# A rewritten instruction order, and one addition of the gate moved from VectorE to an accumulating transfer, in a linear-attention and gated-convolution kernel

## The chip, the cores and the metric

The kernel runs on one core of one Trainium2 chip. The metric is device time in microseconds. Below, PE is the matrix engine (matmuls; its weight loads are shown as PEld), DVE is VectorE, ACT is ScalarE, POOL is GpSimd, and SP is SyncE, which issues transfers.

## The reference

There are two parts, one behind the other. The first is linear attention for 8 batches and 8 heads, with 576 positions and 64 values per head, then an RMS norm per head:

```python
kv = np.einsum('bhsd,bhse->bhde', k, v)
out = np.einsum('bhsd,bhde->bhse', q, kv)
rms = np.sqrt(np.mean(out * out, axis=-1, keepdims=True) + 1e-06)
return (out / rms * g_norm)
```

The heads are put side by side, which gives x with 576 rows of 512 values per batch. The second part is a feed-forward network with a gate:

```python
h = np.maximum(x @ w_in, 0.0)                 # 512 -> 1024
for k in range(3):                            # hp is h with a zero row at either end
    conv_out += conv_w[k][None, None, :] * hp[:, k:k + S, :]
gate = 1.0 / (1.0 + np.exp(-conv_out))
return (h * gate @ w_out)                     # 1024 -> 512
```

## The kernel before

Features lie on partitions and positions run along the free axis from the norm on. The 1024 features of h are 8 blocks of 128 (`f`), and the batches go in pairs: most steps of the second part work on two batches at once.

The whole program is one list of steps, `ORDER`, a string of 852 tokens. A token such as `ab.4.2.2` names a function with its arguments (batch 4, two batches, block pair 2, that is blocks 4 and 5), and `@0` gives it a slot: a PSUM bank, a row buffer or a tap buffer. Each step issues its instructions when the list reaches it, and a chain of dependencies keeps every engine's instructions in that order. So the list sets what each engine does next, and an engine waits in order for whatever its next instruction needs. Transfers are issued from queues too: the loads of q, k, v and the weights on POOL (`Lq`, `Lk`, `Lv`, `Li`, `Lo`), the stores and the transposing transfers on SP (`st`, `sh`, `tq`, `kx`).

The steps that matter below:

- `kv` and `kz` build k^T v on PE; `kva` and `kvd` copy it to SBUF as `kvb`, on ACT or on DVE (the same function `kvc`, L414 and L416). `ot` and `ox` multiply with q.
- The norm of batches 0 to 3: `sq` squares on ACT (L509), `on` or `oq` sums the squares on PE with a matrix of ones (`on` with whole 128-row matmuls, L528; `oq` with four of 64 rows, L537), `nl` takes the reciprocal root on ACT (L545), `mo` multiplies on DVE (L556).
- The norm of batches 4 to 7 is done for two batches at a time: `ss` sums the squares on PE, `ln` takes the reciprocal root on ACT (L574), `sl` makes of it two bf16 parts on DVE, the tile `wparts` (L581 to L584), `sp` spreads these on PE over the rows (L593, with the matrix `spread`), and `mu` multiplies on DVE (L599).
- `hk`, `hs`, `hm` are x @ w_in on PE; `rp`, `rh`, `re` apply the relu on ACT (L665, L640, L619).
- The gate: `ta` multiplies one block of h by the outer two weights of the convolution on DVE (L681 and L682, into the two halves of a tap buffer `taps`), `aa` adds the two products of two blocks, shifted against each other (L687), `ab` adds h (L692, whose weight has been divided out), `sg` takes the sigmoid on ACT (L698), `mg` multiplies h by it (L722). There are two tap buffers.
- `om` is the product with w_out on PE (L732, 8 matmuls of 512 columns per tile of 128 rows, mostly given as two steps of four), `ea` or `ed` copies a tile to a row buffer, on ACT (L738) or DVE (L743), and `st` stores it. The last tile goes in two halves (`oh` L757, `eh` L767, `sh` L777). `fi` are filler matmuls on zeros (L286).

Of the kernel before, what the change touches and what calls it, by code (L numbers as in the profile page):

```python
# [54 lines left out]
AL = mybir.AluOpType  # L55
# [4 lines left out]
pre@0,1 af cad.q.0.0@0 cad.v.0.0@0 fi.10.512@0 qt.0.0.0@2 qd.0.0.0@0 gt.k.1.0 Li.0.4 fi.9.512@0 ct@0 Lq.1.0.2@1  # L60
Lk.1.0.2@0 Lv.1.0.2@1 Li.4.4 ps pg fi.4.512@1 cad.k.1.0@1 caa.v.1.0 caa.k.0.0 kv.0.0.1@4 kva.0.0.1@0 ot.0.0.0@6 pc
cad.v.3.0 cad.k.2.0 fi.2.512@0 cad.k.3.0 caa.q.1.0 qt.0.1.0@2 qd.0.1.0@1 sq.0.0.0@0 oq.0.0.0@4 fi.2.512@0 dg.1
caa.v.2.0 kv.0.1.1@0 fi.2.512@2 nl.0.0.0@0 kva.0.1.1 ot.0.1.0@4 sq.0.1.0@1 cad.q.0.1 qt.0.0.1@2 qa.0.0.1 fi.2.512@0
oq.0.1.0@0 nl.0.1.0@1 mo.0.0.0@0 cad.q.1.1 qt.0.1.1@6 qd.0.1.1 mo.0.1.0 ot.0.0.1@2 sq.0.0.1@2 ot.0.1.1@6 fi.1.512@0
sq.0.1.1@3 oq.0.0.1@0 nl.0.0.1@2 fi.1.512@4 fi.1.512@4 hk.0.1.0.0@4 hk.0.1.0.1 rp.1.0@0 on.0.1.1@0 nl.0.1.1@3
hk.0.2.0.0@5 hk.0.2.0.1 rp.2.0 dg.3 mo.0.0.1 dg.2 hk.0.3.0.0@4 hk.0.3.0.1 hk.0.0.0.0@2 hk.0.0.0.1 rp.0.0 hk.0.0.1.0@3
rp.3.0 hk.0.1.1.0@5 hk.0.3.1.0@0 mo.0.1.1 hk.0.3.1.1 rp.3.1 hk.0.1.1.1 rp.1.1 hk.0.0.1.1 rp.0.1 dg.0 hk.0.2.1.0@1
hk.0.2.1.1 qt.1.0.0@6 kv.1.0.1@4 rp.2.1 cv.0.2@2 sc.0.2@0 cv.0.3@0 qd.1.0.0@2 kvd.1.0.1@1 ot.1.0.1@6 sc.0.3 pl
sq.1.0.1@4 cv.0.1@4 cv.0.0@2 Lq.1.2.2 Lk.1.2.2 Lv.1.2.2 sc.0.1@1 fi.2.512@0 qt.1.1.0@0 qd.1.1.0@3 mg.0.1.1 Lo.0.8
sc.0.0 mg.0.1.0 oq.1.0.1@4 nl.1.0.1@4 mo.1.0.1@1 fi.1.512@2 hk.0.5.1.0@2 hk.0.5.0.0@3 hk.0.5.0.1 rp.5.0 hk.0.5.1.1  # L70
rp.5.1 ta.0.1.5@0 hk.0.4.1.0@0 hk.0.4.1.1 rp.4.1 hk.0.7.0.0@1 hk.0.7.0.1 kv.1.1.1@4 kvd.1.1.1 rp.7.0 ot.1.0.0@2
sq.1.0.0@5 hk.0.7.1.0@6 hk.0.7.1.1 rp.7.1 ta.0.1.7@1 ot.1.1.1@0 sq.1.1.1@6 oq.1.0.0@4 nl.1.0.0@5 mo.1.0.0 hk.0.4.0.0@6
hk.0.4.0.1 rp.4.0 hk.0.6.1.0@7 hk.0.6.1.1 rp.6.1 oq.1.1.1@4 nl.1.1.1@6 mo.1.1.1 hk.0.6.0.0@6 Lq.2.0.4@2 hk.0.6.0.1
rp.6.0 ta.0.1.4 hk.1.6.1.0@7 ta.0.1.6 hk.1.0.1.0@2 ot.1.1.0@4 sq.1.1.0@7 aa.0.1.2 hk.1.1.1.0@3 hk.1.2.1.0@6 hk.1.6.1.1
rh.1.6.1 hk.1.1.1.1 rh.1.1.1 on.1.1.0@0 nl.1.1.0@7 mo.1.1.0 hk.1.2.1.1 hk.1.5.1.0@7 hk.1.5.1.1 rh.1.5.1 rh.1.2.1
hk.1.3.1.0@3 hk.1.3.1.1 rh.1.3.1 hk.1.0.1.1 rh.1.0.1 ab.0.1.2 sg.0.1.5 sg.0.1.4 qt.2.1.0@0 qt.2.0.0@6 hk.1.5.0.0@3
hk.1.5.0.1 rh.1.5.0 qd.2.0.0@4 hk.1.0.0.0@2 hk.1.4.1.0@4 hk.1.4.1.1 hk.1.0.0.1 hk.1.1.0.0@5 hk.1.6.0.0@6 hk.1.1.0.1
hk.1.2.0.0@7 hk.1.2.0.1 rh.1.2.0 rh.1.1.0 rh.1.0.0 hk.1.6.0.1 rh.1.6.0 aa.0.1.3 qd.2.1.0@0 ab.0.1.3 sg.0.1.7 sg.0.1.6
hk.1.7.0.0@0 mg.0.1.2 hk.1.7.1.0@1 hk.1.7.1.1 rh.1.7.1 hk.1.7.0.1 rh.1.7.0 ta.1.1.1@0 ta.1.1.0 Lk.2.0.4@1 Lv.2.0.4@0
Lq.3.0.4@0 Lk.3.0.4@0 Lv.3.0.4@1 Lq.4.0.4@1 aa.1.1.0 hk.1.4.0.0@3 om.0.1.0.4@2 rh.1.4.1 hk.1.4.0.1 rh.1.4.0  # L80
om.0.2.0.4@5 kv.2.0.2@6 mg.0.1.3 om.0.1.4.4 ab.1.1.0 sg.1.1.0 sg.1.1.1 kvd.2.0.2@2 ot.2.0.1@0 sq.2.0.1@0 ed.0.1@0
# [57 lines left out]
def kernel(  # L139
# [685 lines left out]
```

## Time and profile before

| | before |
|---|---|
| median of three runs | 177.59 us (177.56 to 177.61) |
| span of the profiled execution | 175.6 us |
| what lies around the span, median less span | 1.99 us |
| PE busy | 167.9 us (96%) |
| DVE busy | 149.5 us (85%) |
| ACT busy | 148.9 us (85%) |
| POOL busy | 22.2 us (13%) |
| clock granted to PE | full speed in all slices |

The profile shows one execution. Its own time outside the span was not given apart, so the span stands beside the median. A profile row of a group reads: line, engine, operation, output <- input with its shape, count, then the busy total in us and the mean of one in ns, then the idle time of that engine just ahead and what ended it. A row of the timeline starts with its time from the start of the span and its length. A row of a stretch of time gives its start and end, its length, and the busy time of PE, PEld, DVE, ACT and POOL with their instructions, then the granted clock, the mean share of the DMA engines and GB/s.

### The profile page before, as it was taken

The numbers are of one execution on the slowest core, as the hardware profiler recorded it, in microseconds if no ns is written. First come the engines' busy times: TensorE is split into PE (matmuls) and PEld (weight loads), VectorE is DVE, ScalarE is ACT, GpSimd is POOL, SyncE is SP. The second block draws the span as 40 slices with busy tenths as digits, with TensorE's granted clock in tenths as the row PEclk, the third lists the DMA queues.
The fourth block names the chain that finished last, engine by engine and source line by source line (L and its number), as shares of the span: only waits on it lengthen the run. The fifth ranks groups of instructions, "written<-read, shape, count | busy, mean of one in ns | idle before, by whom it ended". The sixth has DMA issues, their size and how long they took to land.

```text
span 175.6 us, 5070 instructions
## 1 busy us (share of the span) xinstructions
PE 167.9 (96%) x2097; PEld 100.0 (57%) x2114; DVE 149.5 (85%) x290; ACT 148.9 (85%) x268; POOL 22.2 (13%) x35
## 2 busy tenths in 40 slices
PE   7979999999999999999999999999999999999992
PEld 2334766676447677644467764444877744444451
DVE  2796638899688899999999998989999999999950
ACT  2368899999978999999999998999999967676721
POOL 3094512200603013030000000000000000000000
PEclk9999999999999999999999999999999999999999
DMA  5999999999999999999999050330310003064486
GB/s 159 392 323 207 207 207 207 208 208 209 207 241 230 227 207 207 170 182 197 258 181 161 14 134 0 119 123 0 119 63 0 0 0 116 13 239 175 179 304 237
DMA packets 25911, 29.11 MB, mean 166 GB/s; under 512 B 6036, under 2 KB 20384, under 8 KB 25888
## 3 DMA queue, kind: packets, MB, share of 16 engines
q0 software_dynamic: 13296, 14.50, 49.2%
q1 hardware_dynamic: 12048, 13.11, 26.2%
q10 hardware_dynamic: 544, 1.18, 1.7%
q8 instruction: 16, 0.26, 0.6%
q14 instruction: 7, 0.06, 0.1%
HBM read 32.52 MB, written 9.44 MB: 239 GB/s over the span
## 4 chain that ended last, share of the span: by engine, by line
PE 76%; DVE 12%; ACT 5%; DMA 3%; issue 3%; ACTq 0%; DVEq 0%
PE banks L732 32%; PE banks L628 14%; PE banks L613 9%; PE banks L658 4%; DMA stg<-in_v_dram 3%; PE banks L460 3%; DVE h L722 2%; PE banks L708 2%; ACT taps L698 2%; PE banks L402 2%; PE banks L593 2%; PE banks L433 1%; PE banks L528 1%; DVE taps L681 1%; PE banks L286 1%
## 5 line engine op out<-in xcount | busy, mean ns | idle before, releaser
L732 PE MATMUL banks<-w_out_sb,h 128*128 128x512 bf16 x267 | 62.8, 379 | 1.2 <-issue 0.6
L698 ACT ACTIVATE taps<-taps,cw 128x576 bf16<-128x576 bf16 (+1 forms) x44 | 40.6, 958 | 5.7 <-DVE taps L692 5.5
L732 PEld LDWEIGHTS <-h 128*128 128x128 bf16 x280 | 26.2, 98 | 30.0 <-issue 1.1
L628 PE MATMUL banks<-x,w_in_sb 128*128 128x288 bf16 (+2 forms) x256 | 34.2, 286 | 0.0
L640 ACT ACTIVATE h<-banks 128x288 bf16<-128x288 f32 (+2 forms) x80 | 29.5, 460 | 0.3 <-PE banks L658 0.2
L628 PEld LDWEIGHTS <-w_in_sb 128*128 128x128 bf16 x256 | 24.4, 98 | 7.8 <-issue 0.8
L722 DVE TENSOR_TENSOR h<-h,taps 128x1152 bf16<-128x1152 bf16 (+1 forms) x24 | 22.8, 952 | 1.2 <-ACT taps L698 1.2
L687 DVE TENSOR_TENSOR taps<-taps 128x1152 bf16<-128x1152 bf16 (+1 forms) x22 | 21.5, 978 | 0.5
L509 ACT ACTIVATE sq<-banks 128x576 bf16<-128x576 f32 (+2 forms) x32 | 20.8, 691 | 1.1 <-PE banks L460 1.1
L692 DVE TENSOR_TENSOR taps<-taps,h 128x1152 bf16<-128x1152 bf16 (+1 forms) x22 | 21.4, 972 | 0.3
L681 DVE TENSOR_SCALAR taps<-h,cw 128x576 bf16<-128x576 bf16 (+1 forms) x44 | 18.7, 424 | 0.6 <-ACT h L665 0.5
L682 DVE TENSOR_SCALAR taps<-h,cw 128x576 bf16<-128x576 bf16 (+1 forms) x44 | 18.4, 418 | 0.0
L738 ACT ACTIVATE row<-banks 128x512 f32<-128x512 f32 x23 | 13.5, 597 | 5.7 <-PE banks L732 4.2
L658 PE MATMUL banks<-x,w_in_sb 128*128 128x288 bf16 (+2 forms) x128 | 17.7, 286 | 0.1
L613 PE MATMUL banks<-x,w_in_sb 128*128 128x288 bf16 x128 | 16.9, 286 | 0.0
L556 DVE SCALAR_TENSOR_TENSOR x<-banks,cw,rs 128x576 bf16<-128x576 f32 (+2 forms) x16 | 13.0, 816 | 3.9 <-ACT rs L545 3.6
L658 PEld LDWEIGHTS <-w_in_sb 128*128 128x128 bf16 x128 | 12.0, 98 | 4.4 <-issue 0.5
L227 ACT ACT_TABLE_LOAD x10 | 12.8, 1283 | 2.0 <-issue 1.8
L613 PEld LDWEIGHTS <-w_in_sb 128*128 128x128 bf16 x128 | 12.3, 98 | 3.7 <-issue 0.2
L443 DVE COPY qT<-banks 128x1152 bf16<-128x1152 bf16 (+2 forms) x13 | 8.8, 681 | 5.7 <-PE banks L433 5.7
L545 ACT ACTIVATE rs<-banks,eps_sb 128x576 f32<-128x576 f32 (+2 forms) x16 | 11.8, 740 | 1.1 <-PE banks L528 1.1
L599 DVE SCALAR_TENSOR_TENSOR x<-o,cw,banks 128x576 bf16<-128x576 f32 (+2 forms) x16 | 12.1, 810 | 0.7 <-PE banks L593 0.5
(89 smaller groups left out, 162.9 us busy)
## 6 DMA issues: line engine op xcount, KB each, us to landing
out_dram<-row SPq DMA_DIRECT2D x35, 256.0 KB, 2.3
q_sb<-in_q_dram POOLq DMA_DIRECT2D x6, 576.0 KB, 17.9
k_sb<-in_k_dram POOLq DMA_DIRECT2D x6, 576.0 KB, 14.5
v_sb<-in_v_dram POOLq DMA_DIRECT2D x6, 576.0 KB, 17.9
stg<-in_v_dram ACTq DMA_DIRECT2D x2, 576.0 KB, 6.2
stg<-in_k_dram SPq DMA_DIRECT2D x4, 288.0 KB, 6.9
w_in_sb<-in_moe_w_in_dram POOLq DMA_DIRECT2D x2, 512.0 KB, 9.9
w_out_sb<-in_moe_w_out_dram POOLq DMA_DIRECT2D x1, 1024.0 KB, 15.5
```

The costliest lines, as they stand in the source:

```text
L509: nc.scalar.activation(T["sq", b, u, s], T["o", b, u, s], AX.Square)
L613: nc.tensor.matmul(ps[:, s, :HS], w_in_sb[:, t, f * P:(f + 1) * P], T["x", b][:, t, c0:c1], start=(t == 0), stop=(t == NT - 1))
L628: nc.tensor.matmul(ps, w_in_sb[:, t, f * P:(f + 1) * P], T["x", b][:, t, c0:c1], start=(t == 0), stop=(t == NT - 1))
L640: nc.scalar.activation(h, fr, AX.Relu)
L658: nc.tensor.matmul(T[at], w_in_sb[:, t, f * P:(f + 1) * P], T["x", b][:, t, c0:c1], start=(t == 0), stop=(t == NT - 1))
L681: nc.vector.tensor_scalar_mul(tap[:, 0, f % 2, :n, 8:8 + S], h[:, f], cw[:, f:f + 1])
L682: nc.vector.tensor_scalar_mul(tap[:, 1, f % 2, :n, :S], h[:, f], cw[:, 2 * NF + f:2 * NF + f + 1])
L687: nc.vector.tensor_add(tap[:, 1, :, :n, :S], tap[:, 0, :, :n, 7:7 + S], tap[:, 1, :, :n, 1:1 + S])
L692: nc.vector.tensor_add(y, y, span(b, n)[:, 2 * j:2 * j + 2])
L698: nc.scalar.activation(y, y, AX.Sigmoid, scale=cw[:, NF + f:NF + f + 1])
L722: nc.vector.tensor_mul(h, h, tap_of(b, j)[:, 1, :, :n, :S])
L732: nc.tensor.matmul(T["om", p, m], h[:, f, m * P:(m + 1) * P], w_out_sb[:, f, :], start=(f == 0), stop=(f == NF - 1))
```

## The change

The list is replaced. Counted as a set, the two lists differ in few steps: two `oq` of batch 1 become `on`; the copies of kv of batches 2 and 3 go from `kvd` to `kva`; `aa.4.2.2` becomes `ad.4.2.2`; ten output copies change engine (`ea.1.6`, `ea.1.2`, `ea.1.8`, `ea.3.5`, `ea.3.6` become `ed`; `ed.2.8`, `ed.3.3`, `ed.3.0`, `ed.3.7`, `ed.3.4` become `ea`), with 12 `ed` and 23 `ea` in both. All other steps are the same, in another order; fillers too.

`ad` adds the two tap products of one block pair for two batches by a transfer from POOL's queue, SBUF to SBUF, 128 partitions of 2304 bf16 values (576 KB), which adds to what stands at its destination. The destination is the first product, where `aa` writes over the second. So the following steps take their operand from `y_of`. The destination reaches into a column that holds a zero for other uses, and `mg` writes the zero again. `on` and `oq` take one PSUM bank where their two results fit in one. The functions `ff`, `dw` and `df` are new and not in the list; they are left out here.

```diff
 ORDER = """
-...kv.2.0.2@6 mg.0.1.3 om.0.1.4.4 ab.1.1.0 sg.1.1.0 sg.1.1.1 kvd.2.0.2@2...
+...kv.2.0.2@4 ta.1.1.1 aa.1.1.0 ab.1.1.0 rh.1.4.1 om.0.2.0.4@3 mg.0.1.3 kva.2.0.2@0...
-...ta.4.2.7@1 ta.4.2.6 aa.4.2.3 ab.4.2.3 om.1.7.4.4 ea.1.7@3 ta.4.2.5
-aa.4.2.2 ab.4.2.2 sg.4.2.4 sg.4.2.5 sg.4.2.7 sl.6@1 sp.6.1.1.6@6...
+...ta.4.2.4@0 ta.4.2.5 mg.2.2.3...ta.4.2.7@1 ta.4.2.6
+ad.4.2.2 ed.1.8@0 ea.1.0@1 aa.4.2.3...ed.1.2@2...ab.4.2.3 ed.1.6@3 om.1.1.0.4@7 om.1.1.4.4 ab.4.2.2...sl.6@0 sp.6.1.1.6@0...
 """
...
+    def pair(n):
+        if 2 * n <= 512:
+            return bank()[:, :2 * n].rearrange("p (e n) -> p e n", e=2)
+        return bank2()[:, :, :n]
...
+    ADS = {tuple(int(a) for a in tok.split("@")[0].split(".")[1::2]) for tok in ORDER.split() if tok.startswith("ad.")}
...
     def on(b, u, s):
         c0, c1 = cols(b, s)
-        ps = T["on", b, u, s] = bank2()[:, :, :c1 - c0]
+        ps = T["on", b, u, s] = pair(c1 - c0)
...
     @op
+    def ad(b, n, j):
+        tap = tap_of(b, j)
+        T["y", b, j] = tap[:, 0, :, :n, 7:7 + S]
+        nc.gpsimd.dma_start(out=T["y", b, j], in_=tap[:, 1, :, :n, 1:1 + S], accum_op=AL.add)
+
+    def y_of(b, n, j):
+        if ("y", b, j) not in T:
+            T["y", b, j] = tap_of(b, j)[:, 1, :, :n, :S]
+        return T["y", b, j]
+
+    @op
     def ab(b, n, j):
-        y = tap_of(b, j)[:, 1, :, :n, :S]
+        y = y_of(b, n, j)
         nc.vector.tensor_add(y, y, span(b, n)[:, 2 * j:2 * j + 2])
...
-        y = tap_of(b, f // 2)[:, 1, f % 2, :n, :S]
+        y = y_of(b, n, f // 2)[:, f % 2]
         nc.scalar.activation(y, y, AX.Sigmoid, scale=cw[:, NF + f:NF + f + 1])
...
     def mg(b, n, j):
         h = span(b, n)[:, 2 * j:2 * j + 2]
-        nc.vector.tensor_mul(h, h, tap_of(b, j)[:, 1, :, :n, :S])
+        nc.vector.tensor_mul(h, h, y_of(b, n, j))
+        if ADS & {(b, j)}:
+            nc.vector.memset(tap_of(b, j)[:, 0, :, :n, 7:8], 0.0)
```

**DVE, from the gating of batches 2 and 3 to the norm factors of batches 6 and 7.** A row gives the line, the operation, output <- input, the size, and the engines or transfers that it waits for. In the kernel before, from `mg.2.2.3` on (`taps_72` and `taps_73` are the two tap buffers):

```order
L722 TENSOR_TENSOR h<-h,taps_73 128x2304 [waits Activation_49]
L681 TENSOR_SCALAR taps_73<-h,cw 128x2x576
L682 TENSOR_SCALAR taps_73<-h,cw 128x2x576 [waits DVE_49]
L681 TENSOR_SCALAR taps_73<-h,cw 128x2x576 [waits Activation_49]
L682 TENSOR_SCALAR taps_73<-h,cw 128x2x576
L687 TENSOR_TENSOR taps_73<-taps_73 128x4x576 [waits DVE_49]
L692 TENSOR_TENSOR taps_73<-taps_73,h 128x4x576 [waits DVE_49]
L681 TENSOR_SCALAR taps_72<-h,cw 128x2x576
L682 TENSOR_SCALAR taps_72<-h,cw 128x2x576
L687 TENSOR_TENSOR taps_72<-taps_72 128x4x576 [waits DVE_49]
L692 TENSOR_TENSOR taps_72<-taps_72,h 128x4x576 [waits DVE_49]
L581 CAST hi<-rs 128x320 [waits Activation_49]
```

In the changed kernel the same stretch, with the lines of the new file (L764 is the gating, L712 and L713 the products, L718 the first addition, L734 the second, L787 `ed`, L594 the first step of `sl`; the buffers are now `taps_74` and `taps_75`):

```order
L764 TENSOR_TENSOR h<-h,taps_75 128x2304 [waits Activation_49]
L712 TENSOR_SCALAR taps_75<-h,cw 128x2x576
L713 TENSOR_SCALAR taps_75<-h,cw 128x2x576 [waits DVE_49]
L712 TENSOR_SCALAR taps_75<-h,cw 128x2x576 [waits Activation_49]
L713 TENSOR_SCALAR taps_75<-h,cw 128x2x576
L787 COPY row<-banks 128x512 [waits DMAHW6_49,DMAHW5_49,PE_49]
L718 TENSOR_TENSOR taps_75<-taps_75 128x4x576 [waits DVE_49]
L787 COPY row<-banks 128x512 [waits DMAHW2_49,PE_49]
L734 TENSOR_TENSOR taps_75<-taps_75,h 128x4x576 [waits DVE_49]
L787 COPY row<-banks 128x512 [waits DMAHW3_49,PE_49]
L734 TENSOR_TENSOR taps_74<-taps_74,h 128x4x576 [waits DMASW5_49]
L594 CAST hi<-rs 128x320 [waits Activation_49]
```

The second pair of products of the other buffer (`ta.4.2.5`) has moved ahead of the gating, the addition L687 of that buffer is gone, three output copies stand between the rest, and the second addition on `taps_74` waits for a transfer of POOL's queue (DMASW).

**PE, where the norm factors are spread.** Before, the last weight load and matmul of `om.1.7.4.4`, then the first spreading matmuls:

```order
L732 LDWEIGHTS h
L732 MATMUL banks<-w_out_sb,h 128x512
L593 LDWEIGHTS spread [waits DVE_49]
L593 MATMUL banks<-wparts,spread 128x256 [waits Activation_49]
L593 LDWEIGHTS spread
L593 MATMUL banks<-wparts,spread 128x256
```

In the changed kernel (L776 is `om`, L624 is `sp`) the spreading comes behind `om.1.4.4.4`:

```order
L776 MATMUL banks<-w_out_sb,h 128x512
L624 LDWEIGHTS spread [waits DVE_49]
L624 MATMUL banks<-wparts,spread 128x256 [waits Activation_49]
L624 LDWEIGHTS spread
L624 MATMUL banks<-wparts,spread 128x256
L624 LDWEIGHTS spread
L624 MATMUL banks<-wparts,spread 128x256 [waits Activation_49]
L624 LDWEIGHTS spread
L624 MATMUL banks<-wparts,spread 128x256
L776 LDWEIGHTS h
L776 MATMUL banks<-w_out_sb,h 128x512
```

The four matmuls of `om.1.7.4.4`, which stood ahead of the spreading, now stand behind its first four matmuls.

**ACT, in batch 3's norm.** Before (L545 is `nl`, L509 `sq`, L640 `rh`):

```order
L545 ACTIVATE rs<-banks,eps_sb 128x2x288 [waits PE_49]
L509 ACTIVATE sq<-banks 128x2x288 [waits DVE_49,PE_49]
L640 ACTIVATE h<-banks 128x288 [waits PE_49]
L545 ACTIVATE rs<-banks,eps_sb 128x2x288 [waits DVE_49,PE_49]
L640 ACTIVATE h<-banks 128x288 [waits DMAHW1_49,DMAHW0_49,PE_49]
```

In the changed kernel (L558, L522 and L671 are these, L429 is `kva.3.0.2`):

```order
L558 ACTIVATE rs<-banks,eps_sb 128x2x288 [waits PE_49]
L522 ACTIVATE sq<-banks 128x2x288 [waits DVE_49,PE_49]
L429 ACTIVATE kvb<-banks 128x256 [waits PE_49]
L671 ACTIVATE h<-banks 128x288 [waits PE_49]
L558 ACTIVATE rs<-banks,eps_sb 128x2x288 [waits DVE_49,PE_49]
L671 ACTIVATE h<-banks 128x288 [waits DMAHW1_49,DMAHW0_49,PE_49]
```

The copy of kv stands ahead of a relu and a reciprocal root that PE's next steps wait for. On POOL the loads of batches 4 to 7 come in another order (q of batch 5 ahead of v and k of batch 4, q of batch 7 behind k and v of batch 6, v of batch 7 ahead of its k), and the accumulating transfer is the last in the queue. On SP the stores of the first eight row tiles and the transposing transfers of batches 6 and 7 are interleaved in another way.

More of the change, by code (lines that the diff above doesn't have):

```diff
@@ L65 @@
[L65 to L69, printed above, removed]
@@ L286, in fi, with ff @@
             nc.tensor.matmul(ps[:, :w], zero[:, :P], zero[:, :w], start=True, stop=True)
+    @op
+    def ff(n, w):
+        ps, z = bank(), zero.bitcast(FP32)
+        for _ in range(n):
+            nc.tensor.matmul(ps[:, :w], z[:, :P], z[:, :w], start=True, stop=True)
     @op
@@ L408, in kvc @@
     def kvc(eng, b, u0, n):
-        if u0 == 0:
+        if ("kvb", b) not in T:
             T["kvb", b] = ring("kvb", [P, 2, 2 * D], BF16, "kvb")
@@ L584, in sl, with dw, df, h_of @@
         nc.vector.scalar_tensor_tensor(w, hi, nb[:, 0:1], r, op0=AL.mult, op1=AL.add)
+    @op
+    def dw(b0):
+        T["rd", b0] = dram.tile([P, GW], FP32, name="rd")
+        nc.sync.dma_start(out=T["rd", b0], in_=T["rs", b0])
+    @op
+    def df(b, u, s, b0):
+        w, c = width(b, s), 2 * (b - b0) + s
+        to = T["sp", b, u, s] = ring("qkv"[(4 * (b - b0) + 2 * u + s) % 3], [P, 2, 320], FP32, "spread")[:, :, :w]
+        fr = T["rd", b0].rearrange("(t c i) w -> c i t w", t=NT, i=2)[c, :, 2 * u:2 * u + 2, :w]
+        for i in range(2):
+            nc.sync.dma_start(out=to[half(i)], in_=fr[i].unsqueeze(0).to_broadcast([D, 2, w]))
+    def h_of(b, f):
+        if ("h", b // 2) not in T:
+            T["h", b // 2] = ring("h", [P, NF, 2, S], BF16, "h")
+        return T["h", b // 2][:, f, b % 2, :]
     @op
```

151 lines of the change are left out of this document (79 added, 72 removed).

## The prediction, made before the changed kernel ran

> **What bounds the kernel now.** I read the page first, then the busy times by stage, then the matrix engine's waits, then the chain that ended last.
>
> ```profile
> span 175.6 us, 5070 instructions
> PE 167.9 (96%) x2097; PEld 100.0 (57%) x2114; DVE 149.5 (85%) x290; ACT 148.9 (85%) x268; POOL 22.2 (13%) x35
> ```
>
> The runs have a median of 177.59 us and the span is 175.6, so 1.99 us lies around the span; I take that as unchanged and make the sum against 177.59. PE is busy for 96% of it. The two engines that the change unloads, DVE and ACT, have 85% each, but an average over stages says little, so here are the stages (length, then the busy time of PE, PEld, DVE, ACT, POOL, the granted clock, the DMA share and GB/s):
>
> ```profile
> 29.00:172.27 143.27, 141.64 (x1697) 85.33 (x1694) 131.50 (x222) 128.47 (x234) 10.37 (x14) 1.00 0.72 149
> 50.00:55.00 5.00, 5.00 (x109) 2.91 (x108) 3.46 (x6) 3.56 (x8) 1.48 (x2) 1.00 1.18 240
> 57.00:105.00 48.00, 47.46 (x776) 31.04 (x779) 46.33 (x74) 47.87 (x86) 3.70 (x5) 1.00 1.07 178
> 105.00:118.30 13.30, 13.05 (x95) 5.96 (x96) 11.97 (x17) 12.78 (x23) 0.00 (x0) 1.00 0.22 80
> 141.00:172.30 31.30, 31.03 (x150) 14.72 (x151) 27.86 (x57) 19.52 (x35) 0.00 (x0) 1.00 0.42 157
> ```
>
> The old and new orders put the same steps on every engine up to about 29 us, so the first row is all that the change can touch: PE is idle in it for 143.27 - 141.64 = 1.63 us. PE's work is the same in both, so 177.59 - 1.63 = 176.0 is the floor. Losses have no such bound, because from 57 to 105 us ACT is busy for 47.87 of 48.00 and DVE for 46.33: three engines are full together there, and work added to ACT has nowhere to go. From 141 us on ACT has slack (19.52 of 31.30) and PE none.
>
> The waits of PE's two queues in that stretch (total, times, longest), and the end of the chain (start, length):
>
> ```profile
> PEld L593 <- DVE wparts L584: 0.5, 1, 0.5
> PE banks L732 <- issue: 0.6, 4, 0.2
> ...
> 162.94 7.50 PE banks L732 x34
> 170.44 1.76 PE banks L757 x16
> 172.27 0.38 ACT row L767
> ```
>
> One wait of 0.5 stands out: the spreading matmuls (L593) that need the norm factors `wparts` of batches 6 and 7. It is the place where the change does most. The tail is the matrix engine's last 9 us, one ACT copy and a store; the new order has the same work there, so I put nothing on it.
>
> **The change part by part.** The groups with their durations (total, mean ns of one):
>
> ```profile
> L687 DVE TENSOR_TENSOR taps<-taps 128x2304 bf16<-128x2304 bf16 x8 | 10.9, 1361 | 0.2
> L743 DVE COPY row<-banks 128x512 f32<-128x512 f32 x12 | 8.2, 687 | 1.6 <-PE banks L732 1.6
> L738 ACT ACTIVATE row<-banks 128x512 f32<-128x512 f32 x23 | 13.5, 597 | 5.7 <-PE banks L732 4.2 <-issue 1.4
> L414 DVE CAST kvb<-banks 128x256 bf16<-128x256 f32 x6 | 2.5, 422 | 0.4 <-PE banks L479 0.2
> L665 ACT ACTIVATE h<-banks 128x256 bf16<-128x256 f32 x8 | 3.5, 455 | 0.4 <-PE banks L658 0.4
> L272 DVE MEMSET taps<- 128x4 bf16 x2 | 0.1, 62 | 0.0
> ```
>
> 1. *Work between 105 and 118 us.* DVE loses one addition of taps, 1.361, and one ACT copy of an output row (L738) after another, three in all, comes to DVE: 3 x 0.687 = 2.06. With the memset of 0.062 DVE has 2.06 + 0.06 - 1.36 = 0.76 more there, and ACT 3 x 0.597 = 1.79 less. So the transfer does not unload DVE in this stage; it pays for the copies.
>
> 2. *Where `wparts` comes out.* DVE's rows there (start, length, idle before), and PE's:
>
> ```profile
> 104.89 0.51 DVE L681 TENSOR_SCALAR taps<-h,cw 128x1152 bf16<-128x1152 bf16 x1
> 105.32 0.51 DVE L682 TENSOR_SCALAR taps<-h,cw 128x1152 bf16<-128x1152 bf16 x1
> 106.50 1.36 DVE L722 TENSOR_TENSOR h<-h,taps 128x2304 bf16<-128x2304 bf16 x1 [0.67 <-ACT taps L698]
> 107.78 0.51 DVE L681 TENSOR_SCALAR taps<-h,cw 128x1152 bf16<-128x1152 bf16 x1
> ...
> 109.61 1.36 DVE L687 TENSOR_TENSOR taps<-taps 128x2304 bf16<-128x2304 bf16 x1
> 111.01 1.36 DVE L692 TENSOR_TENSOR taps<-taps,h 128x2304 bf16<-128x2304 bf16 x1
> 112.29 0.51 DVE L681 TENSOR_SCALAR taps<-h,cw 128x1152 bf16<-128x1152 bf16 x1
> ...
> 116.30 0.33 DVE L581 CAST hi<-rs 128x320 bf16<-128x320 f32 x1 [0.28 <-ACT rs L574]
> ...
> 117.61 0.55 DVE L584 SCALAR_TENSOR_TENSOR wparts<-hi,nb,rs 128x320 bf16<-128x320 bf16 x1
> 117.16 1.03 PE L732 MATMUL banks<-w_out_sb,h 128*128 128x512 bf16 x4
> 118.22 0.42 PE L593 MATMUL banks<-wparts,spread 32*128 32x256 bf16 x6
> 118.58 0.39 PE L732 MATMUL banks<-w_out_sb,h 128*128 128x512 bf16 x1
> ```
>
> In the new order the second pair of tap products stands ahead of the gating at 106.50, in the 0.67 that DVE waits for ACT there. Products step by 0.43 (104.89 to 105.32), so the two pairs end at 104.89 + 4 x 0.43 = 106.61 and the gating starts then. Behind it come, by steps of these rows: gating 1.28 (106.50 to 107.78), two pairs 1.83 (to 109.61), addition 1.40 (to 111.01), second addition 1.28 (to 112.29), and the three copies, 2.06: together 7.85. At 106.61 + 7.85 = 114.46 DVE reaches the second addition on the transferred sum, and with 1.36 for it, 115.82, the first norm cast, which started at 116.30 before. So `wparts`, done at 117.61 + 0.55 = 118.16 before, comes 0.48 earlier, at 117.68. The norm's own input isn't later: ACT has lost 1.79 ahead of it.
>
> PE gets there earlier still, since four matmuls of L732 now stand behind the first spreading matmuls instead of ahead. Four take 1.03 and a lone one 0.39, so they step by (1.03 - 0.39) / 3 = 0.21, and four steps are 0.85. Note how the wait of 0.5 reads: it is one of weight loads; the matmuls before it end at 117.16 + 1.03 = 118.19, and the spreading starts at 118.22, so PE itself lost 0.03. Now PE is there at 118.22 - 0.85 = 117.37 and waits until 117.68: 0.31 lost in place of 0.03, +0.3 us. PE is full behind it, so it keeps that loss.
>
> 3. *The transfer itself.* No accumulating transfer is in the trace. It is the last in POOL's queue, so nothing waits behind it there; on DVE the second addition waits for it, and behind that the norm factors, and then PE. It may start when the second pair of products is done, 106.61, and has the 7.85 of item 2 as cover. The nearest rows are a small SBUF to SBUF copy and a store (KB each, us from issue to landing), a load in the crowded middle, and the time of POOL's issues:
>
> ```profile
> kvx<-kvb SPq DMA_DIRECT2D x2, 32.0 KB, 1.8
> ...
> out_dram<-row SPq DMA_DIRECT2D x6, 256.0 KB, 2.3
> k_sb<-in_k_dram POOLq DMA_DIRECT2D x1, 576.0 KB, 12.3
> L347 POOL DMA_DIRECT2D k_sb<-in_k_dram x8: 727/740/745, 10.0 to 75.0; - x8
> 75.00:80.00 5.00, 5.00 (x35) 2.00 (x34) 5.00 (x8) 5.00 (x11) 1.48 (x2) 1.00 1.28 176
> ```
>
> It moves 576 KB. From the first two rows 224 KB more cost 0.5, so 576 KB would land in 2.3 + 0.7 = 3.0; that is the low end. The load of the same size took 12.3, in a stage with the engines at a DMA share of 1.07; between 105 and 118 us the share is 0.22 (row above), so that is the far end and little like it. I take 1.8 plus two passes over the data, the sum being read and written, at the 0.5 per 224 KB of those rows: 1.8 + 2 x 1.3 = 4.4, and 5.1 with 0.74 for the issue. It is nearest to the quiet rows. All but the far end are under 7.85, so the transfer costs nothing where I take it; each microsecond past 7.85 would cost one.
>
> The Trainium skill, "SBUF - State Buffer", section "Who interferes with whom", says that a VectorE copy or tensor_scalar in a two-port mode holds the port pair that GpSimd needs and blocks it fully. By it the issue could be held behind the four products that follow the gating, 4 x 0.513 = 2.05, and the sum would be unchanged at 5.1 + 2.05 = 7.2, but only just. The trace does not bear it out for issues: POOL's took 727 to 745 ns, also in 75 to 80 us, where DVE is busy for 5.00 of 5.00 and two of them (1.48) fell.
>
> 4. *Copies of kv in batches 2 and 3.* DVE loses 2 x 0.422 and ACT gets two of about 0.455 (the row of L665, same shape). Both come before 57 us. From 50 to 55 us ACT is idle for 5.00 - 3.56 = 1.44, which hides the second and what is left of the first. If that cover is gone, ACT enters its full stage late by up to 0.91, and PE with it. I take 0 and keep 0.91.
>
> 5. *Copies at the end.* Five go from DVE to ACT and two the other way (12 and 23 of each kind, as before, with the three of item 1). From 141 us ACT has 11.78 idle, DVE 3.44: nothing. 6. *Two sums of squares with whole-row matmuls* (`on` for `oq`) take two 288-column passes of 128 rows in place of four half-size ones that run two at a time: nothing. 7. *Loads.* POOL's list has three loads moved ahead of others (q5 before v4 and k4). The far end is a load that lands late: k4 goes behind two loads of 576 KB,
>
> ```profile
> GB/s 159 392 323 207 207 207 207 208 208 209 207 241 230 227 207 207 170 182 197 258 181 161 14 134 0 119 123 0 119 63 0 0 0 116 13 239 175 179 304 237
> ...
> 44.27 0.74 POOL L347 DMA_DIRECT2D k_sb<-in_k_dram  x1 [12.49 <-PE banks L402]
> 66.86 0.78 PE L402 MATMUL banks<-v_sb,k_sb 64*64 64x64 bf16 x72
> ```
>
> each 2.85 at the 207 GB/s of the steady slices, so it lands 5.7 later than at 44.3 + 12.3 = 56.6, at 62.3; its first use is at 66.86: nothing, with 4 us to spare. SP's stores move, but each row buffer is written again far later.
>
> The sum: +0.3 from item 2, less about 0.1, my guess for the small waits on issue (0.6 in all) that another order does not repeat: 177.59 + 0.2 = 177.8. Between 177.23 and 177.95 is within 0.2%, about what a measurement of this kernel can tell from no change.
>
> **The rivals.**
> - *A, forecast: 177.8.* PE waits a little for `wparts`, else all is as full as before. If the copies on DVE take 0.1 less each, the wait is gone: 177.5; if ACT's inputs for them are 0.3 late, 178.1.
> - *B, faster: 176.8.* ACT, lighter by 1.79 ahead of the norm, and DVE, lighter by 0.84 before 57 us, end the small waits of the two full stages: 48.00 - 47.46 = 0.54 and 13.30 - 13.05 = 0.25, and 177.59 - 0.79 = 176.8. For it: a full stage of three engines leaves small gaps that another order can close. Against: 1.63 is all there is, much of it issue.
> - *C, slower: the transfer lands after DVE's cover.* It decides from 7.85 us after 106.61 on. At 8.9 (the issue held up, and element-wise addition slower than two passes) `wparts` and PE are a further 1.0 late: 178.8. This is the case that the page's rule of blocked ports leads to. Against: the quiet DMA of that stage.
> - *D, slower: ACT does not hide the two kv copies.* 177.59 + 0.91 = 178.5. For it: 47.87 of 48.00. Against: the 1.44 idle just before.
>
> **How the numbers follow.** A 0.36, B 0.30, C 0.16, D 0.18. A lies within 0.2%, B is faster, C and D slower: 0.30, 0.36, 0.34. The point is A's. The range goes from 176.6, a little under B, to 178.6, just over D; it leaves out B near its floor (0.08) and most of C (0.1). A's own range is 177.5 to 178.1.
>
> **What would show it.** A: in the changed kernel one wait of PE's loads for `wparts` of 0.5 to 1.2, and a PE gap of about 0.3 ahead of the second group of spreading matmuls; the transfer landing in 3 to 7 us with no DVE wait for it. B: PE's idle in 29 to 172 us under 1 us. C: a DVE wait on the transfer at the second addition of L734, followed by the gap of PE. D: ACT over 47.9 of 48 in the middle and PE waiting for banks that ACT empties. I am wrong most simply if DVE reaches the stage at 105 us earlier or later than before, since item 2 counts from 104.89.

## The result and the profile after

The changed kernel takes 179.84 us (median of four runs, 179.73 to 180.18) beside 177.57 us of the kernel before: a ratio of 1.0132, with a 95% interval of 1.0118 to 1.0145. It is 2.3 us slower. The forecast was 177.8 us with a range of 176.6 to 178.6, so the time lies outside it.

The page of the changed kernel begins:

```profile
span 177.9 us, 5078 instructions
PE 170.4 (96%) x2110; PEld 99.9 (56%) x2110; DVE 147.6 (83%) x288; ACT 149.3 (84%) x270; POOL 24.0 (14%) x36
```

The stages as before (length, then PE, PEld, DVE, ACT, POOL, clock, DMA share, GB/s):

```profile
29.00:172.27 143.27, 141.10 (x1694) 83.98 (x1682) 129.23 (x219) 128.74 (x236) 12.10 (x15) 1.00 0.72 152
57.00:105.00 48.00, 47.64 (x778) 30.49 (x777) 43.40 (x65) 47.42 (x86) 4.11 (x5) 1.00 1.00 183
105.00:118.30 13.30, 13.23 (x97) 5.99 (x95) 12.25 (x21) 11.69 (x19) 1.31 (x1) 1.00 0.51 124
141.00:172.30 31.30, 29.66 (x145) 13.88 (x144) 25.06 (x53) 20.78 (x38) 0.00 (x0) 1.00 0.34 126
```

The middle stages are as full as before. The last one is not: PE is idle there for 31.30 - 29.66 = 1.64 us, where it was 0.27. The waits of PE over the whole run, the largest first:

```profile
PE banks L776 <- ACT row L782: 1.6, 1, 1.6
```

One wait makes the 1.64, and these are its rows, PE first, then ACT:

```profile
155.81 6.42 PE L776 MATMUL banks<-w_out_sb,h 128*128 128x512 bf16 x29
163.87 6.20 PE L776 MATMUL banks<-w_out_sb,h 128*128 128x512 bf16 x28 [1.64 <-ACT row L782]
160.66 0.57 ACT L782 ACTIVATE row<-banks 128x512 f32<-128x512 f32 x1
162.56 0.78 ACT L740 ACTIVATE taps<-taps,cw 128x576 bf16<-128x576 bf16 x1 [1.33 <-DVE taps L734]
163.24 0.58 ACT L782 ACTIVATE row<-banks 128x512 f32<-128x512 f32 x1
```

PE needs the PSUM bank of `om.3.0` for `om.3.2`. The copy `ea.3.0` that frees it (163.24) stands on ACT behind the sigmoid `sg.7.1.6`, and this waits 1.33 us for DVE's second addition `ab.7.1.3`. So ACT stood still with the copy in its queue. And why was DVE late? Some 15 us earlier, DVE and ACT each wait once for the other:

```profile
143.91 1.50 ACT L671 ACTIVATE h<-banks 128x256 bf16<-128x256 f32 x4 [1.14 <-DVE h L764]
...
147.55 0.51 ACT L671 ACTIVATE h<-banks 128x256 bf16<-128x256 f32 x1
148.10 0.76 DVE L764 TENSOR_TENSOR h<-h,taps 128x1152 bf16<-128x1152 bf16 x1 [1.56 <-ACT h L671]
```

The relu `rh.7.4.1` (143.91) waits for the gate product `mg.6.1.2`, and then `mg.6.1.0` (148.10) waits 1.56 us for the relu `rh.7.0.1` (147.55). Neither pair shares a value: the relus write batch 7, the gate products batch 6. But the two batches lie interleaved by block in one tile, so the two blocks of a gate product enclose a block of the other batch, and the program's synchronisation lets the later of the two in the list wait for the earlier one (experiment 2 turns both pairs around). In the list before, each pair stands in the same order, but far apart: `rh.7.0.1` 21 tokens ahead of `mg.6.1.0` and `rh.7.4.1` 75 behind `mg.6.1.2`, so the wait is over long before it matters. In the new list the distances are 2 and 7.

The rest of the 2.3 us is small. Where both kernels have the same work behind them, PE begins the next matmuls here, before and after (the `ox` products, then the output product of batches 4 and 5):

```profile
107.68 0.33 PE L500 MATMUL banks<-qT,kvb 64*64 64x320 bf16 x4
140.92 2.32 PE L732 MATMUL banks<-w_out_sb,h 128*128 128x512 bf16 x9
```

```profile
108.03 0.33 PE L513 MATMUL banks<-qT,kvb 64*64 64x320 bf16 x4
141.35 1.89 PE L776 MATMUL banks<-w_out_sb,h 128*128 128x512 bf16 x8
```

That is 0.35 late at 108 us and 0.43 at 141. The last chain then adds the 1.64.

### The profile page after: what moved, and what is told of

Its sections match the earlier page's. It is cut to its first block, busy times and chain, and to the rows that moved or that the text cites. A ratio compares the mean times of both kernels' runs of the same rounds, so it can differ in the third digit from the quotient of the medians.

```text
span 177.9 us, 5078 instructions
## 1 busy us (share of the span) xinstructions
PE 170.4 (96%) x2110; PEld 99.9 (56%) x2110; DVE 147.6 (83%) x288; ACT 149.3 (84%) x270; POOL 24.0 (14%) x36
## 4 chain that ended last, share of the span: by engine, by line
PE 60%; ACT 20%; DVE 15%; issue 3%; ACTq 0%
PE banks L776 20%; PE banks L689 8%; PE banks L659 7%; PE banks L293 7%; ACT taps L740 6%; ACT h L671 5%; PE banks L644 4%; DVE h L764 4%; DVE taps L718 3%; PE banks L473 3%; PE banks L446 2%; DVE taps L713 2%; DVE taps L734 2%; DVE taps L712 2%; ACT sq L522 2%
## 5 line engine op out<-in xcount | busy, mean ns | idle before, releaser
L776 PE MATMUL banks<-w_out_sb,h 128*128 128x512 bf16 x280 | 65.3, 380 | 1.7 <-ACT row L782 1.6
L776 PEld LDWEIGHTS <-h 128*128 128x128 bf16 x280 | 26.0, 98 | 31.6 <-issue 3.6
L671 ACT ACTIVATE h<-banks 128x288 bf16<-128x288 f32 (+2 forms) x80 | 30.0, 464 | 1.9 <-DVE h L764 1.1
L764 DVE TENSOR_TENSOR h<-h,taps 128x1152 bf16<-128x1152 bf16 (+1 forms) x24 | 22.8, 952 | 2.7 <-ACT h L671 1.6
L522 ACT ACTIVATE sq<-banks 128x576 bf16<-128x576 f32 (+2 forms) x32 | 20.8, 684 | 1.7 <-PE banks L473 1.0
L734 DVE TENSOR_TENSOR taps<-taps,h 128x1152 bf16<-128x1152 bf16 (+1 forms) x22 | 21.2, 968 | 0.2
L718 DVE TENSOR_TENSOR taps<-taps 128x1152 bf16<-128x1152 bf16 (+1 forms) x21 | 20.0, 956 | 0.5
L712 DVE TENSOR_SCALAR taps<-h,cw 128x576 bf16<-128x576 bf16 (+1 forms) x44 | 19.0, 432 | 0.1
L713 DVE TENSOR_SCALAR taps<-h,cw 128x576 bf16<-128x576 bf16 (+1 forms) x44 | 18.9, 430 | 0.0
L293 PE MATMUL banks<-zero 128*128 128x512 bf16 x37 | 12.5, 464 | 1.2 <-DVE zero L272 1.2
```

What stands on the lines that cost most here:

```text
L293: nc.tensor.matmul(ps[:, :w], zero[:, :P], zero[:, :w], start=True, stop=True)
L522: nc.scalar.activation(T["sq", b, u, s], T["o", b, u, s], AX.Square)
L671: nc.scalar.activation(h, fr, AX.Relu)
L712: nc.vector.tensor_scalar_mul(tap[:, 0, f % 2, :n, 8:8 + S], h[:, f], cw[:, f:f + 1])
L718: nc.vector.tensor_add(tap[:, 1, :, :n, :S], tap[:, 0, :, :n, 7:7 + S], tap[:, 1, :, :n, 1:1 + S])
L734: nc.vector.tensor_add(y, y, span(b, n)[:, 2 * j:2 * j + 2])
```

## The experiments

Two theories stood against each other. Theory 1: the copies that went from DVE to ACT at the end were wrongly placed. Theory 2: DVE was late because of the pair of waits on `h`, and the copy only showed it.

**1. The copy ahead of the sigmoid.**

```diff
-ea.3.3@0 sg.7.1.6 om.3.1.0.4@1 om.3.1.4.4 ea.3.0@1 sg.7.1.7
+ea.3.3@0 om.3.1.0.4@1 om.3.1.4.4 ea.3.0@1 sg.7.1.6 sg.7.1.7
```

> The changed kernel with one exchange on ScalarE: the copy ea.3.0, which frees the PSUM bank that om.3.2 waits for, stands ahead of the sigmoid sg.7.1.6 instead of behind it. In the changed kernel ScalarE waits 1.33 us for DVE's ab.7.1.3 with that copy queued behind, and PE loses 1.64 us. Theory 1 (the place of the copy is the cause): the 1.64 us come back, 178.2 us. Theory 2 (DVE itself is late, and the copy only shows it): the last gate product mg.7.1.2 still ends at 167.5 us of the span, PE would want it for om.3.5 at 166.3, so a new wait of 1.2 us replaces the old one: 179.4 us.

Measured: 179.28 us (ratio to before 1.0086, 95% interval 1.0067 to 1.0106; the figures in brackets below are the same two things). Only 0.56 of the 1.64 came back, as theory 2 had it. PE's rows and its loads' wait show what took the place of the old wait:

```profile
164.38 4.93 PE L776 MATMUL banks<-w_out_sb,h 128*128 128x512 bf16 x20 [0.48 <-ACT row L782]
PEld L776 <- DVE h L764: 0.5, 1, 0.5
```

```profile
166.59 0.76 DVE L764 TENSOR_TENSOR h<-h,taps 128x1152 bf16<-128x1152 bf16 x1 [0.24 <-ACT taps L740]
```

The two together are about 1.0: PE again waits for a bank and for the last gate product (the third row), which DVE ends only at 166.59 + 0.76 = 167.35.

**2. Both pairs of relu and gate product turned around.** The gate product `mg.6.1.0` now stands ahead of the relu `rh.7.0.1`, and the relu `rh.7.4.1` ahead of the gate product `mg.6.1.2`. (Later expectations call this "the gate products ahead of the relus", which names the first pair only.) The order on every engine stays; only who waits for whom changes.

```diff
-mg.6.1.2 hs.7.1.0@0 hs.7.4.1@4 hs.7.3.1@6 om.2.2.0.4@3 om.2.2.4.4 ab.6.1.0 rh.7.4.1
+hs.7.1.0@0 hs.7.4.1@4 hs.7.3.1@6 om.2.2.0.4@3 om.2.2.4.4 rh.7.4.1 mg.6.1.2 ab.6.1.0
...
-rh.7.0.1 om.2.4.0.4@0 mg.6.1.0
+om.2.4.0.4@0 mg.6.1.0 rh.7.0.1
```

> The changed kernel, with the same order on every engine; only the program's place of three steps differs, so that the gate product mg.6.1.0 no longer waits for the relu rh.7.0.1 (same blocks, other batch, no value in common), and the relu rh.7.4.1 no longer waits for mg.6.1.2. In the changed kernel these are DVE's wait of 1.56 us at 146.5 and ScalarE's of 1.14 us at 142.8. Theory 2 (DVE is late at the end because of this pair of waits): DVE's chain comes about 1.3 us earlier and PE's wait of 1.64 us all but vanishes: 178.3 us. Theory 1 (the copy's place alone): DVE's chain has slack before, so the copy is still behind a late sigmoid: 179.5 us or more.

Measured: 178.22 us (1.0023, 1.0010 to 1.0036), and 178.26 us on another chip, where the run was repeated:

> The kernel with the gate products ahead of the relus once more, beside the next one on the same chip: 178.2 us if chips agree; 178.9 to 179.2 us if the other chip's last store lands later, as in the run with the kv copies back on VectorE.

So 1.6 of the 2.3 us hang on these two waits. DVE begins `mg.6.1.0` without a wait (146.73, where it was 148.10), and the relu `rh.7.0.1` on ACT now waits for it:

```profile
146.73 0.75 DVE L764 TENSOR_TENSOR h<-h,taps 128x1152 bf16<-128x1152 bf16 x1
147.52 0.50 ACT L671 ACTIVATE h<-banks 128x256 bf16<-128x256 f32 x1 [0.60 <-DVE h L764]
```

From 149.63 us on PE runs 87 of these matmuls without a gap, past the place where it had stood still:

```profile
149.63 19.07 PE L776 MATMUL banks<-w_out_sb,h 128*128 128x512 bf16 x87
```

**3. The addition back on DVE**, in the changed kernel.

```diff
-ta.4.2.6 ad.4.2.2 ed.1.8@0
+ta.4.2.6 ed.1.8@0
...
-ab.4.2.2 om.1.4.0.4@5
+aa.4.2.2 ab.4.2.2 om.1.4.0.4@5
```

> The changed kernel with the addition of blocks 4 and 5 of batches 4 and 5 back on VectorE (aa.4.2.2 right ahead of ab.4.2.2), all else in the new order. If the transfer takes 1.36 us off the path to the norm factors: these come at 119.0 in place of 117.6, PE waits 1.1 us for them, and DVE is later up to the end too: 180.9 us. If VectorE had slack there: 179.8 us, no change.

Measured: 180.56 us (1.0155, 1.0137 to 1.0172), 0.72 us more than the changed kernel. PE waits as expected, and the wait at the end stays what it was:

```profile
118.80 0.29 PE L624 MATMUL banks<-wparts,spread 32*128 32x256 bf16 x4 [1.12 <-DVE wparts L597]
PE banks L776 <- ACT row L782: 1.6, 1, 1.6
```

The transfer is worth 0.7 us in the new order. It is less than the 1.12 because PE reached the spreading earlier in this execution, at 118.80 - 1.12 = 117.68 us, where it was 117.88 in the changed kernel, and the rest is closed up in PE's work behind it: the last chain begins 0.84 later (142.19 and 141.35).

**4. The transfer alone**, in the kernel before. The file is that of the changed kernel with the old list, so its choice of PSUM banks in `on` and `oq` comes along.

```diff
-ta.4.2.4@0 mg.2.2.3
+ta.4.2.4@0 ta.4.2.5 mg.2.2.3 ad.4.2.2
...
-ta.4.2.5 aa.4.2.2 ab.4.2.2
+ab.4.2.2
```

> The kernel before with the transfer alone: the old order, but the second pair of products ahead of the gate product as in the change, and the addition of blocks 4 and 5 of batches 4 and 5 by the accumulating transfer. The transfer landed 5.8 us after its issue in the changed kernel, so DVE reaches the second addition at about 112.4 and waits 0.6 us; the norm factors then wait for ScalarE's root as before. Theory 'PE is the bound there': 177.5 us, no change. Rival 'VectorE was the bound': up to 1.4 us faster, 176.2 us.

Measured: 177.83 beside 177.71 us (1.0004, 0.9995 to 1.0014): no change. DVE waits 0.59 for the transfer, then 1.81 for ACT's root:

```profile
113.19 1.36 DVE L734 TENSOR_TENSOR taps<-taps,h 128x2304 bf16<-128x2304 bf16 x1 [0.59 <-DMA taps<-taps]
116.37 0.33 DVE L594 CAST hi<-rs 128x320 bf16<-128x320 f32 x1 [1.81 <-ACT rs L587]
```

**5. The kv copies back on DVE**, on top of experiment 2, and once more beside it.

```diff
-kva.2.0.2@0 ... kva.3.0.2@0
+kvd.2.0.2@0 ... kvd.3.0.2@0
```

> The changed kernel with the gate products ahead of the relus (178.22 us when run alone), and also the two copies of kv of batches 2 and 3 back on VectorE. Where the changed order loses its other 0.3 to 0.4 us before 107 us of the span: if on ScalarE, which has these copies (0.9 us) ahead of its full stage, 177.9 us; if in PE's own order (more changes between kinds of matmul), no change, 178.2 us.

> The kernel with the kv copies back on VectorE once more. Its profile showed PE's end 0.07 us earlier than without that, but the span 0.7 us longer: the last store was issued at 173.8 in both and landed 0.75 us later. If that belongs to the kernel: 179.2 us and 1.0 above the run beside it. If it belongs to the chip: the same as the run beside it.

Measured: 179.20 us (1.0086, 1.0072 to 1.0100) and 179.19 us (1.0076, 1.0050 to 1.0101), 0.9 above the run beside it. I had expected 177.9 or no change. PE is not what got slower: the last store was issued 0.06 us earlier than in experiment 2 in the first profiles (173.47 and 173.53) and 0.10 later in the repeated ones (173.31 and 173.21), where the two profiles of experiment 2 alone differ by 0.32. The loss lies behind PE's end and is the subject of the last section. So these copies cost PE nothing that shows on either engine.

**6. The spreading behind `om.1.7.4.4` again**, on top of experiment 2.

```diff
-sp.6.1.1.6@0 sp.7.0.1.6@2 mu.7.0.1@0 mu.6.1.1@1 om.1.7.4.4 sp.7.1.1.6@2
+om.1.7.4.4 sp.6.1.1.6@0 sp.7.0.1.6@2 mu.7.0.1@0 mu.6.1.1@1 sp.7.1.1.6@2
```

> The changed kernel with the gate products ahead of the relus, and the four matmuls of om.1.7.4.4 back ahead of the first spreading matmuls. The changed kernel showed no PE wait for the norm factors where the prediction put 0.3 us, since PE came there 0.6 us late. If the place of the spreading costs nothing now: 178.2 us, or 178.1 with one change of kind less. If the later spreading (0.85 us) makes the next norm products and relus late: 178.6 us.

Measured: 179.16 us (1.0080, 1.0068 to 1.0093), worse by 0.9 than experiment 2, and for a reason that I hadn't named. The third spreading needs the PSUM banks of the second, and without the four matmuls between them PE waits until DVE has emptied these:

```profile
119.93 0.32 PE L624 MATMUL banks<-wparts,spread 32*128 32x256 bf16 x4 [0.92 <-DVE x L630]
```

**7. The last output copies on their old engines**, in the changed kernel.

```diff
-ea.2.8@2 ... ea.3.3@0 ... ea.3.0@1 ... ed.3.5@0 ... ea.3.7@1 ... ea.3.4@3 ... ed.3.6@0
+ed.2.8@2 ... ed.3.3@0 ... ed.3.0@1 ... ea.3.5@0 ... ed.3.7@1 ... ed.3.4@3 ... ea.3.6@0
```

> The changed kernel with the seven output copies of the last two row groups on the engines that they had before (2.8, 3.3, 3.0, 3.7, 3.4 on DVE, 3.5 and 3.6 on ScalarE), in the new order. If it was wrong to give these copies to ScalarE, the 1.64 us of PE's wait come back: 178.2 us. If DVE is late at the end because of its wait of 1.56 us at 146.5, three more copies of 0.69 ahead of the last gate product make it 2.1 later, and PE waits up to 3 us in all: 180.5 to 181.4 us.

Measured: 180.84 us (1.0194, 1.0168 to 1.0220), 1.0 slower than the changed kernel. Theory 1 falls: with DVE late, giving it more copies makes it later.

```profile
PE banks L776 <- DVE row L787: 2.5, 2, 2.1
```

**8 and 9. Two output copies into DVE's idle time**, in the kernel of experiment 4; both have the products `ta.4.2.7` and `ta.4.2.6` moved ahead of the first copy, and `aa.4.2.3` ahead of the second.

```diff
-ea.1.6@5 ... ea.1.2@1
+ed.1.6@5 ... ed.1.2@1     (run 8)
-ea.1.6@5 ... ea.1.8@3
+ed.1.6@5 ... ed.1.8@3     (run 9)
```

> The kernel before with the transfer alone (177.83 beside 177.71 us), where DVE idled 0.59 us for the transfer and 1.81 us for ScalarE's root; now the output copies 1.6 and 1.2 go from ScalarE to DVE, into that idle time. The root comes about 1.1 us earlier on ScalarE and with it the norm factors. If the wait for these (0.5 us of weight loads, 0.03 to 0.1 of PE) and ScalarE's full stage behind it held PE back: 177.3 us. If PE alone is the bound: no change, 177.7 us.

Measured: 178.15 us (1.0025, 1.0015 to 1.0034). DVE reached the second copy late, and PE waited for its bank:

```profile
PE banks L513 <- DVE row L787: 0.3, 1, 0.3
```

> As the run that moved the output copies 1.6 and 1.2 to DVE in the kernel before with the transfer alone (178.15 beside 177.70 us), but 1.6 and 1.8: the copy 1.2 on DVE kept PE waiting 0.3 us for its PSUM bank, and the bank of 1.8 is needed 2 us later. If that bank was its whole loss: 177.7 to 177.8 us. If the norm factors, 1 us earlier, are worth something to PE: 177.4 us.

Measured: 177.68 beside 177.66 us (0.9995, 0.9982 to 1.0007). That wait is gone and nothing is won. But the factors did not come earlier either, so the run doesn't say what that would be worth. ACT, with two copies less, now waits for PE ahead of the last squares, and the last step of `wparts` starts at 117.53, where it was 117.61 before:

```profile
112.18 1.68 ACT L522 ACTIVATE sq<-banks 128x512 bf16<-128x512 f32 x3 [0.29 <-PE banks L513]
117.53 0.55 DVE L597 SCALAR_TENSOR_TENSOR wparts<-hi,nb,rs 128x320 bf16<-128x320 bf16 x1
```

No version here beats the kernel before.

**10. The same kind of wait put into the kernel before.**

```diff
-hs.7.0.1@6 rh.7.0.1 hs.6.1.0@4
+hs.7.0.1@6 hs.6.1.0@4
...
-sg.6.1.1 mg.6.1.0 ab.6.1.1 om.2.1.0.4@4 om.2.2.0.4@2 om.2.2.4.4 ea.2.2@1
+sg.6.1.1 om.2.1.0.4@4 om.2.2.0.4@2 om.2.2.4.4 ea.2.2@1 rh.7.0.1 mg.6.1.0 ab.6.1.1
```

> The kernel before with one relu (rh.7.0.1) moved on ScalarE behind the copy ea.2.2 and ahead of the gate product mg.6.1.0, which then waits for it as in the changed kernel; the orders of DVE and PE are the same. DVE comes to mg.6.1.0 at 146.6 us of the span and the relu ends at about 147.2, so DVE is 0.6 us later from there on. Theory 2 (from 141 us on DVE has no slack, and what it loses PE loses at the last gate products): 178.2 to 178.3 us. If DVE has slack there: 177.7 us.

Measured: 178.24 beside 177.66 us (1.0027, 1.0013 to 1.0042), as theory 2 had it. DVE loses 0.52 us at the product, and PE gets it at the end as one wait for a bank and one for a gate product:

```profile
147.32 0.76 DVE L722 TENSOR_TENSOR h<-h,taps 128x1152 bf16<-128x1152 bf16 x1 [0.52 <-ACT h L640]
PE banks L732 <- ACT row L738: 0.3, 1, 0.3
PEld L732 <- DVE h L722: 0.4, 1, 0.4
```

## Why the prediction was wrong

- **What bounds the kernel.** Right: PE is full up to 141 us in both, and all that was lost is PE's idle time and its small delays. Rival B's sign, less than 1 us of PE idle between 29 and 172 us, did not come: it is 143.27 - 141.10 = 2.17 us.
- **Item 1 and 2, the norm factors.** The end of the sum held, in part by luck. DVE reached the second addition on the transferred sum at 114.50 (predicted 114.46) and ended `wparts` at 117.06 + 0.55 = 117.61 (117.68):

```profile
114.50 1.35 DVE L734 TENSOR_TENSOR taps<-taps,h 128x2304 bf16<-128x2304 bf16 x1
115.77 0.31 DVE L594 CAST hi<-rs 128x320 bf16<-128x320 f32 x1
...
117.06 0.55 DVE L597 SCALAR_TENSOR_TENSOR wparts<-hi,nb,rs 128x320 bf16<-128x320 bf16 x1
117.88 0.29 PE L624 MATMUL banks<-wparts,spread 32*128 32x256 bf16 x4
```

  But DVE began later and needed less than was said. The gating began at 107.06 and not at 106.61, since DVE still waited 0.27 for ACT's sigmoid, and from there to 114.50 it took 7.44 us and not 7.85, since a copy steps by 0.60 (110.16 to 110.76) where 0.687 was taken, and the addition behind it by 1.27 where 1.40 was:

```profile
107.06 1.36 DVE L764 TENSOR_TENSOR h<-h,taps 128x2304 bf16<-128x2304 bf16 x1 [0.27 <-ACT taps L740]
110.16 0.68 DVE L787 COPY row<-banks 128x512 f32<-128x512 f32 x1
110.76 1.34 DVE L718 TENSOR_TENSOR taps<-taps 128x2304 bf16<-128x2304 bf16 x1
112.03 0.68 DVE L787 COPY row<-banks 128x512 f32<-128x512 f32 x1
```

  The +0.3 of PE did not come: I let PE arrive on time, and it came 0.35 late already, so the factors were there. Experiment 3, with the factors later, shows that the place is as tight as was said.
- **Item 3, the transfer.** Right in sum, a little short in size: 5.8 us from issue to landing where 5.1 was taken (the sign of rival A, 3 to 7 us, held). It began 0.75 later than was said (107.36 and not 106.61) and still landed at 107.36 + 5.8 = 113.2, ahead of the addition at 114.50; no wait for it shows on DVE, and rival C did not occur. POOL's issue took 1.31 us in place of the 0.74 of most loads:

```profile
taps<-taps POOLq DMA_DIRECT2D x1, 576.0 KB, 5.8
107.36 1.31 POOL L724 DMA_DIRECT2D taps<-taps  x1 [30.30 <-ACT taps L740]
```

  By the rule of the Trainium skill that the prediction weighed ("SBUF - State Buffer", "Who interferes with whom") this issue could have been held for 2.05, an estimate from the product rows. The extra was 0.57, with a gate product and, in its last 0.34 us, a tap product running on DVE beside it. In experiment 4 products ran beside the last 0.73 us of the issue, more than twice as long, and it took 1.34. So the length hardly follows the products, and most of the extra is more likely of the transfer's form; that is argued, not shown. The prediction was wrong, though, that the trace speaks against such blocking for plain issues: the two issues at 75 us that it named ran beside a cast and a tap addition, and only the last 0.06 us beside a product. In the changed kernel two load issues fell beside products of 128x1152. They took 0.94 and 0.96 us (at 70.37 and 75.35), and products beside issues up to 0.84 where 0.51 is usual:

```profile
75.35 0.96 POOL L360 DMA_DIRECT2D v_sb<-in_v_dram  x1 [4.04 <-PE banks L473]
75.93 0.65 DVE L713 TENSOR_SCALAR taps<-h,cw 128x1152 bf16<-128x1152 bf16 x1
76.50 0.84 DVE L712 TENSOR_SCALAR taps<-h,cw 128x1152 bf16<-128x1152 bf16 x1
```

  That agrees with the rule in direction.
- **Item 4, the kv copies.** Zero for PE was right (experiment 5); rival D, 0.91, did not occur.
- **The zero for everything behind 141 us (item 5 and the sentence on the tail) is the step that failed.** It was argued from idle time and from the work being the same: ACT has 11.78 us idle from 141 us on. That was so (20.78 of 31.30 busy after), but an engine in order isn't free while it waits: the copy stood behind a sigmoid that waited for DVE, and PE behind the copy, 1.64 us, where the prediction had nothing. The choice of engine for these copies, which item 5 was about, was not the fault: with the old engines the changed kernel is 1.0 us slower (experiment 7). The cause under it was in no item. My list of what the change moves had copies, loads and additions, but not the relus of batch 7, which the new order brings close to gate products of batch 6 in the same tile; the order shows them, and I read it only at three places. Experiment 2 gives 1.6 us back by turning these two waits around, and experiment 10 makes the kernel before 0.6 us slower by one of them.
- **The size of what was left to lose.** The prediction noted PE's floor of 176.0 and that losses have no bound, and yet gave slower only 0.34, with no mechanism behind 141 us. It had the row for it: DVE with 27.86 of 31.30 busy there, and PE with 0.27 to spare.
- **What stays open.** After experiment 2, 0.5 us are left (178.22 beside 177.71). Part of it arises before the `ox` products near 108 us. Where PE is at a given step differs between two profiles of one kernel (108.30 and 107.96 in those of experiment 2), so it is better counted from PE's first product with w_out:

```profile
41.10 1.03 PE L732 MATMUL banks<-w_out_sb,h 128*128 128x512 bf16 x3
41.14 1.03 PE L776 MATMUL banks<-w_out_sb,h 128*128 128x512 bf16 x4
```

  From there to the `ox` products PE takes 107.68 - 41.10 = 66.58 us before and 108.03 - 41.14 = 66.89 in the changed kernel; over the nine profiles of the new order it is 66.73 to 66.97. The largest single waits of PE between 29 and 160 us are 0.2. Experiment 5 rules out the kv copies (66.97 and 66.96 with them on DVE, 66.90 and 66.88 in experiment 2), and the place of the spreading isn't it, since moving it back in experiment 6 wins nothing and costs the 0.92 of a new wait. A different sequence of kinds of matmul, with its small gaps, is what is left; that is argued, not shown.

## What to carry to other kernels

Before you call a moved instruction free because its engine has idle time, ask what stands ahead of it in that engine's order and what that waits for: a copy behind a waiting sigmoid is as late as the sigmoid. When two batches or stages lie interleaved in one tile, writes that share no value can still be made to wait for each other; which of them comes first in the program then decides who waits, and turning that around costs nothing in the engines' orders. Where two engines and PE are all full, a wait early on shows up far away, here 15 us later and on a third engine, so follow the late engine back to its last idle gap before blaming the place where PE stops.

## What the runs showed of the hardware

Experiment 5 was slower by 0.9 us though its last store was issued at most 0.1 later. Between 174 and 176 us its DMA queues hold a packet of instruction fetch that the kernel of experiment 2 doesn't have in the same window (both from the repeated runs, that of experiment 5 first):

```profile
GB/s 246 369 532 205 349 328 328 328 369 369 307 451 123 41 0 0 0 20 20 20 0 20 0 0 20 0 0 20 20 20 0 0 0 0 0 0 0 0 0 0
...
q1 hardware_dynamic: 202, 0.22, 32.3%
q14 instruction: 1, 0.01, 1.0%
```

```profile
GB/s 492 287 328 308 369 307 348 389 348 287 123 62 0 0 0 0 0 0 0 0 0 0 0 0 0 0 0 0 0 0 0 0 0 0 0 0 0 0 0 0
...
q1 hardware_dynamic: 185, 0.18, 26.4%
```

In experiment 5 the store's bulk ends 0.1 us later, as it was issued, but a trickle of packets follows it for 0.8 us: the slices at 20 GB/s. The span grew by as much (177.0 against 176.2), and both profiles of that kernel show it. So the 0.9 us of experiment 5 are no price that PE pays for the kv copies; nearly all of it lies in the landing of the last store.

Why the packets trickle stays open. The last 3 us of the traces show a short trickle (0.1 to 0.3 us) in the kernel before and in experiments 4, 8 and 9, one of 0.6 us in experiment 10, and none in the changed kernel and experiments 1, 2, 3, 6 and 7. Each kernel with a trickle has seven packets of instruction fetch in its run, each of the others six, but for experiment 7, which has seven and no trickle. That the extra fetch and the trickle belong together fits all but one of these; no run tested it by itself. In experiment 10 PE ends 0.6 us later too (172.80 where it was 172.19), which is what its medians differ by (178.24 - 177.66), so its verdict doesn't rest on the trickle.
